# Moving operands of TensorE 128 bytes beyond their stationary ones, modulo 256 bytes, in a three-stage network on one core

## The chip, the cores and the metric

The kernel runs on one core of a Trainium2 chip. The metric is the time of one execution in microseconds, as the device measures it. 1132.77 us is the median of three executions of the kernel before.

## The reference, cut to what matters

Three stages follow each other, for a batch of 2 with 3136 tokens and 256 features. Everything is float32.

```python
# attention: z is 64 wide, v and u are 256 wide
scores = (1.0 / S) * np.matmul(z, z.transpose(0, 2, 1))
attn = np.maximum(scores, 0.0) ** 2
x = u * np.matmul(attn, v)
# layer 1: a token mix of rank 32, then a feed-forward block 256 -> 1024 -> 256
h = x.transpose(0, 2, 1) @ U @ V
u = x + h.transpose(0, 2, 1)
x = u + np.maximum(u @ w_ch1, 0.0) @ w_ch2
# layer 2: a Fourier mix over tokens and features, a normalization, a second block
u = x + np.real(np.fft.fft(np.fft.fft(x, axis=1), axis=2))
un = (u - mean(u)) / np.sqrt(var(u) + 1e-06)
out = u + np.maximum(un @ w_ch1, 0.0) @ w_ch2
```

## The kernel before, in words

Every float32 matrix is split into a high and a low part of type float32r, and a product is the sum of three matmuls: high by high, high by low, low by high. A matmul has a stationary operand (here mostly 128 columns, loaded into the array by an LDWEIGHTS) and a moving one (mostly 448 columns, CH in the code); each matmul loads its own stationary operand, so a load for the next matmul runs beside each matmul.

Tokens go in 7 chunks of 448 per batch element. In attention, `scores` (lines 558 to 595) multiplies blocks of z: stationary KT, moving Q, 64 rows, so that two matmuls, one in the upper and one in the lower half of the array, run side by side as a pair. ScalarE and VectorE make from it the squared scores and split them into `h` and `l`. `products` (lines 599 to 622) multiplies them with the values: stationary Vt, moving `h` and `l`, again in pairs. A chunk has 13 steps, and a full step has 12 pairs of `products` and 3 pairs of `scores`. The 13th block of z has only 64 rows, KTl; its scores are 224 columns wide, the lower half of the array taking the first 224 columns of Q and the upper half the other 224.

In the feed-forward blocks, `hidden` (lines 363 to 376) multiplies the first weights `w` (stationary) with a chunk's `h` and `l`, in six matmuls of 448 columns, and `project` (lines 378 to 397) the second weights with the hidden layer's `Hh` and `Hl`, in another six. Such a step of twelve is repeated 8 times a chunk, for 14 chunks in each layer, and the rest of the program's work (Fourier transforms, normalizations, low-rank sums) is put between these steps by a schedule that is written out by hand. Layer 1's weights are in the pool `wpool`; layer 2's first weights are in `wpool2`, its second ones in `wpool`.

The tiles stand in SBUF one behind the other, pool by pool, in the order in which they are first asked for, without room between them. The sizes of all tiles ahead of a tile therefore set its address. Taken modulo 256 bytes, the address of the moving operand less that of the stationary one (the offset, here) is this when the kernel is built:

| matmuls | moving, stationary | offset before | offset after |
|---|---|---|---|
| attention's scores, line 574 | Q, KT | 0 | 128 |
| the 13th step's scores, lower half, upper half | Q, KTl | 0, 128 | 128, 0 |
| attention's values, line 616 | h or l, Vt | 0 | 128 |
| layer 1, hidden, lines 368 to 370 | h or l, w | 0 | 128 |
| layer 2, hidden, lines 368 to 370 | h or l, w | 64 | 128 |
| both layers, projections, lines 393 to 395 | Hh or Hl, w | 64 | 128 |
| low-rank update, lines 269 and 713 | Vs, Gs | 0 | 128 |
| normalization sums, lines 308 and 327 | sm, ones | 64 | 128 |
| transforms in float32r, lines 956 to 958 and 1013 to 1018 | nh, nl, Th, Tl; b49, fA, fB | 64 | 128 |
| transform in float32, lines 995 and 1005 | f64s; wr, col128 | 64 | 0 |
| low-rank sums in float32, line 234 | xT1, stg or an; Us | 0 to 192 | 0 to 192 |

The 64 in layer 2's hidden matmuls has another origin than that of the projections: there the moving operand is at 0 modulo 256 and the weights are at 192.

The low-rank table `Us` (line 132) holds U for the low-rank sums, `rank_sums` (lines 228 to 238). Its last reader is layer 1's mixer in the middle of the program. `alternating` (lines 926 to 931) makes sums of every second token for the Fourier transform, through a scratch tile `alt` of 1024 bytes per partition.

Of the kernel before, what the change touches and what calls it, by code (L numbers as in the profile page):

```python
# [10 lines left out]
F32 = mybir.dt.float32  # L11
F32R = mybir.dt.float32r
I32 = mybir.dt.int32
# [8 lines left out]
CH = 448  # L22
# [52 lines left out]
def f(ap):  # L75
    return ap.bitcast(F32)
# [3 lines left out]
def program(ctx, tc, zT, v, uT, U, V, w1a, w2a, w1b, w2b, b49, f64, fd, rep, mask, out):  # L80
# [8 lines left out]
    def hcopy(o, i):  # L89
        nc.scalar.copy(o, i)  # L90

    def sub(o, a, b):
        tt(out=o, in0=a, in1=b, op=ALU.subtract)  # L93

    const = ctx.enter_context(tc.tile_pool(name="const", bufs=1))
    com = ctx.enter_context(tc.tile_pool(name="com", bufs=3))
# [34 lines left out]
    ones = const.tile([128, 128], F32R, name="ones")  # L131
    Us = const.tile([128, 26, RANK], F32, name="Us")
    Gs = [const.tile([128, D], F32R, name=f"Gs{b}") for b in range(NB)]

    def constants(t):
        make_identity(nc, ident)
        late_dma(out=repc, in_=rep)
        late_dma(out=maskc[:, 0:7], in_=mask)
        late_dma(out=t[0:98, 0:128], in_=b49)
        late_dma(out=f64s, in_=f64)  # L140
        late_dma(out=t[:, 256:512], in_=fd)
        nc.vector.memset(t[:, 768:896], 1.0 / D)
        for _ in range(3):
            yield
        hcopy(ones, t[:, 768:896])
        for x in (b49h, b49l):
            nc.gpsimd.memset(f(x), 0.0)
        hcopy(b49h[0:98], t[0:98, 0:128])
        sub(b49l[0:98], t[0:98, 0:128], f(b49h[0:98]))
        yield  # L150
        for dst, k in ((fA, 256), (fB, 384)):
            hcopy(dst[:, 0], t[:, k : k + 128])
            sub(dst[:, 1], t[:, k : k + 128], f(dst[:, 0]))
            if dst is fA:
                yield
# [23 lines left out]
    def fetch_w(raw, src, k, second):  # L179
        if second:  # L180
            load(out=raw[:, 0:512], in_=src[k * 128 : k * 128 + 128, :])
        else:
            load(
                out=raw[:, 0:512].rearrange("p (a n) -> p a n", a=2),
                in_=src[:, k * 256 : k * 256 + 256].rearrange("(a p) n -> p a n", p=128),
            )
# [33 lines left out]
    def misc():  # L220
        p, tag = misc_pools[misc_at[0] % len(misc_pools)]
        misc_at[0] += 1
        return p.tile([128, 512], F32, tag=tag, name="ps_" + tag)
# [23 lines left out]
    class Chunk:  # L247
# [2 lines left out]
            self.sl = slice(c * CH, c * CH + CH)  # L250

        def load(self):
            self.vs = com.tile([128, CH], F32R, tag="Vs", name="Vs", bufs=1)
            for k in (0, 64):
                late_dma(out=self.vs[k : k + 64, :], in_=V_d[:, self.sl])

# [142 lines left out]
        def finish(self):  # L399
            b = self.b  # L400
            if self.layer == 1:
                for a in range(2):
                    tt(out=late["xT"][b][:, a, self.sl], in0=self.acc[a][:, 0:CH], in1=self.x[:, a], op=ALU.add)
            else:
                o = c2(ptile())
                if self is chunks[-1]:
                    t0, n = self.c * CH, CH // 2
                    for cuts in (((0, 0, CH),), ((1, 0, n), (1, n, CH))):
                        for a, s, e in cuts:
                            tt(out=o[:, a, s:e], in0=self.acc[a][:, s:e], in1=self.x[:, a, s:e], op=ALU.add)  # L410
                            store = nc.scalar.dma_start if a and s == 0 else load
                            store(out=out[b, a * 128 : a * 128 + 128, t0 + s : t0 + e], in_=o[:, a, s:e])
                    return
                for a in range(2):
                    tt(out=o[:, a], in0=self.acc[a][:, 0:CH], in1=self.rs, op=ALU.mult)
                for a in range(2):
                    tt(out=o[:, a], in0=o[:, a], in1=self.x[:, a], op=ALU.add)
                    load(out=out[b, a * 128 : a * 128 + 128, self.sl], in_=o[:, a])
# [4 lines left out]
    def attention(stack):  # L423
        att = stack.enter_context(tc.tile_pool(name="att", bufs=2))
# [8 lines left out]
        zraw, qraw, vraw = {}, {}, {}  # L433
# [26 lines left out]
                sub(t[:, 1, c : c + 64], raw[:, 0, 0:64], f(t[:, 0, c : c + 64]))  # L460

        def load_q(b, qc):
            t = qraw[b, qc] = att.tile([128, CH], F32, tag="qraw", name="qraw", bufs=1)
            for r in halves[0 : 1 if (b, qc) == (0, 0) else 2]:
                (late_dma if (b, qc) == (0, 1) else load)(out=t[r], in_=zT[b, :, qc * CH : qc * CH + CH])

# [36 lines left out]


        def stage():
            return att.tile([128, 1152], I32, tag="stg", name="stg")

        def conv_U(k):
            raw = stage()
# [223 lines left out]
        t = att.tile([128, 5, D], F32R, tag="an", name="warm", bufs=1).rearrange("p a n -> p (a n)")  # L733
# [7 lines left out]
        for k in range(32):  # L741
            r, n = halves[k % 2], 128 if k < 8 else 352
# [45 lines left out]
        for i in range(-LAG, len(steps)):  # L788
# [3 lines left out]
            if i >= 0:  # L792
                b, qc, p = steps[i]
# [6 lines left out]
                n = i % NP  # L800
# [6 lines left out]
                if (b, qc) == (1, NC - 1):  # L807
                    if p == 2:
                        chunks[0].load()
                        a = att.tile([128, 2, CH], F32, tag="uT", name="uT")  # L810
# [21 lines left out]
    mp = late["mp"] = ctx.enter_context(tc.tile_pool(name="mp", bufs=2))  # L832
# [7 lines left out]
    xT = late["xT"] = [xpool.tile([128, 2, S], F32, tag=f"xT{b}", name=f"xT{b}") for b in range(NB)]  # L840


    raw128 = mp.tile([128, 112], F32, tag="raw128", name="raw128", bufs=1)
    col128 = mp.tile([128, 128], F32, tag="col128", name="col128", bufs=1)
    rows = [mp.tile([128, CH], F32, tag=f"row{k}", name=f"row{k}", bufs=1) for k in range(2)]
    late["half"] = rows[0][:, 0:D]
    y = mp.tile([128, 416], F32, tag="y", name="y", bufs=1)
    top = [mp.tile([98, 32], F32, tag=f"top{b}", name=f"top{b}", bufs=1) for b in range(NB)]
    for t in (raw128, col128, y[:, 392:416]):
        nc.gpsimd.memset(t, 0.0)  # L850
# [8 lines left out]
    def pair_late():  # L859
        nats.append(nats.pop(0))  # L860
        return nats[-1]
# [33 lines left out]
    def halves49(b):  # L895

        nat = {}
        x0, x1 = (xT[b][:, a].rearrange("p (s m r) -> p s m r", m=49, r=2) for a in range(2))
        yv = y[:, 0:392].rearrange("p (s m r) -> p s m r", m=49, r=2)

        def fold(i):

            s0, s1 = 4 * i, 4 * i + 4
            for t0, t1 in ((0, 1), (1, s1)) if s0 == 0 else ((s0, s1),):
                for m, w in ((0, 0), (1, 25), (25, 1)):
                    n = 24 if m else 1
                    in1 = x1[:, t0:t1, w : w + n]
                    if t0:
                        in1 = in1[:, :, :, ::-1]
                    tt(  # L910
                        out=yv[:, t0 - s0 : t1 - s0, m : m + n],
                        in0=x0[:, t0:t1, m : m + n],
                        in1=in1,
                        op=ALU.add,
                    )
            yt = mp.tile([128, 416], F32, tag="A1" if i == 7 else "yt", name="yt", bufs=1)
            nc.vector.transpose(out=yt, in_=y)
            for c in (0, 32, 64, 96):
                (load if c < 64 else late_dma)(
                    out=nat_d[b][i, :, c : c + 32].rearrange("(j t) d -> t j d", t=32),  # L920
                    in_=yt[c : c + 32].rearrange("p (j d) -> p j d", d=32),
                )
            if i == 7:
                load(out=raw128[0:32, 0:98], in_=xT[b][0:1, 1, :].rearrange("o (s p) -> o s p", p=98))

        def alternating(i, x):

            v = x[0:98].rearrange("p (s d r) -> p s d r", s=4, r=2)
            t = mp.tile([98, 4, 64], F32, tag="alt", name="alt", bufs=1)
            sub(t, v[:, :, :, 0], v[:, :, :, 1])  # L930
            nc.vector.reduce_sum(out=top[b][0:98, 4 * i : 4 * i + 4], in_=t, axis=mybir.AxisListType.X)

        def fetch(i):
            h, l = nat[i] = pair_late()
            load(
                out=f(l)[0:98].rearrange("p (s d) -> p s d", s=4),
                in_=nat_d[b][i, 0:392].rearrange("(s p) d -> p s d", p=98),
            )

        def tokens(i):  # L940
            h, l = nat[i]
            hcopy(h[0:98], f(l)[0:98])
            alternating(i, f(l))
            sub(l[0:98], f(l)[0:98], f(h[0:98]))

        def axis49(i):
            ps = misc()
            dft49(ps, *nat.pop(i))
            w = mp.tile([128, 512], F32, tag="wst", name="wst")
            hcopy(w, ps)  # L950
            load(out=scr[b][:, 4 * i : 4 * i + 4, :], in_=w.rearrange("p (s d) -> p s d", s=4))

        return fold, fetch, tokens, axis49

    def dft49(ps, h, l):
        mm(ps, b49h, h, start=True, stop=False)
        mm(ps, b49h, l, start=False, stop=False)  # L957
        mm(ps, b49l, h, start=False, stop=True)  # L958
# [167 lines left out]
    with tc.manual_schedule():  # L1126
# [21 lines left out]
        for i in range(nstep + 2):  # L1148
# [23 lines left out]
            if i in fetches:  # L1172
                b, k0, k1 = fetches[i]
# [57 lines left out]
```

## Time and profile before

| what | value |
|---|---|
| median of three executions | 1132.77 us (1132.64 to 1133.49) |
| the profiled execution's own time | 1132.07 us |
| its span, from the first to the last instruction | 1130.3 us |
| TensorE, matmuls: busy, share of the span | 1125.1 us, 100% |
| VectorE: busy, share | 847.0 us, 75% |
| ScalarE: busy, share | 633.7 us, 56% |
| GpSimd: busy, share | 181.5 us, 16% |
| attention (line 616's last start) | to 536.4 us |
| feed-forward steps of layer 1, then of layer 2 | 536.7 to 835.05 us, then to the end |

In the profile PE is TensorE's matmuls, PEld its weight loads, DVE is VectorE, ACT ScalarE, POOL GpSimd. A matmul's start is measured and its end is modelled, matmuls overlap in the array, and so the time between starts tells the pace, and not the duration that a row gives for one. The chain that ended last goes back from the last instruction to what released each; its shares tell which engine sets the end.

### The profile page before, as it was taken

What the parts mean: (1) busy time and instruction counts of PE and PEld (TensorE: products, weight loads), DVE (VectorE), ACT (ScalarE), POOL (GpSimd) and SP (SyncE); (2) the same over time, 40 slices, a digit from 0 to 9 for tenths busy, and PEclk for the clock granted to TensorE, in tenths of its full rate; (3) what the DMA queues carried; (4) which work ended last, traced back from release to release, by engine and by line L of the source; (5) the groups of instructions that cost most, each with busy time, mean ns of one, the idle gap of its engine ahead of it and who ended that gap; (6) DMA issues with size and microseconds to landing.
All of it is one profiled execution on the core that took longest, in us unless ns stands there. A gap on an engine that the chain in (4) does not pass through costs nothing.

```text
span 1130.3 us, 21424 instructions
## 1 busy us (share of the span) xinstructions
PE 1125.1 (100%) x8310; PEld 1061.7 (94%) x8310; DVE 847.0 (75%) x1571; ACT 633.7 (56%) x1032; POOL 181.5 (16%) x299
## 2 busy tenths in 40 slices
PE   9999999999999999999999999999999999999998
PEld 8999999999999999999989999999999999999997
DVE  8877888888887667676667777577588888777863
ACT  8777777878786666675334444343345444444431
POOL 2202310221022102202221112111131100000010
PEclk9999999999999999999999999999999999999999
DMA  5212322324123302111823455231143321111111
GB/s 168 75 46 61 104 80 69 119 71 127 47 72 118 121 18 59 50 36 32 265 62 95 128 159 130 74 75 45 47 107 100 76 48 42 33 42 33 42 33 42
DMA packets 86758, 88.96 MB, mean 79 GB/s; under 512 B 27398, under 2 KB 76034, under 8 KB 86656
## 3 DMA queue, kind: packets, MB, share of 16 engines
q1 hardware_dynamic: 70272, 58.44, 17.2%
q0 software_dynamic: 16032, 28.93, 10.2%
q8 instruction: 65, 1.06, 0.4%
q14 instruction: 37, 0.30, 0.1%
q10 hardware_dynamic: 352, 0.21, 0.1%
HBM read 57.67 MB, written 29.82 MB: 77 GB/s over the span
## 4 chain that ended last, share of the span: by engine, by line
PE 99%; ACT 0%; DVE 0%; issue 0%; DVEq 0%; POOL 0%; POOLq 0%
PE psO L616 37%; PE psS L574 9%; PE psH L368 8%; PE psH L369 8%; PE psC L394 8%; PE psC L395 8%; PE psH L370 8%; PE psC L393 8%; PE psS L743 0%; PE ps_m L995 0%; PE ps_g L995 0%; PE ps_x L995 0%; PE psS L234 0%; PE ps_g L234 0%; PE ps_m L958 0%; PE ps_m L957 0%
## 5 line engine op out<-in xcount | busy, mean ns | idle before, releaser
L616 PE MATMUL psO<-h,Vt 64*128 64x448 f32 x2744 | 345.1, 363 | 0.2 <-DVE h L585 0.2
L616 PEld LDWEIGHTS psO<-h,Vt 64*128 64x128 f32 x2744 | 294.4, 185 | 9.1 <-DVE h L585 0.7
L93 DVE TENSOR_TENSOR l<-P,h 128x896 fp32r<-128x896 f32 (+2 forms) x237 | 224.8, 954 | 33.3 <-ACT h L90 16.4
L373 ACT ACTIVATE Hh<-psH 128x448 fp32r<-128x448 f32 x224 | 121.0, 541 | 201.5 <-PE psH L370 198.3
L374 DVE SCALAR_TENSOR_TENSOR Hl<-psH,Hh 128x448 fp32r<-128x448 f32 x224 | 138.3, 620 | 117.9 <-ACT Hh L373 115.7
L590 ACT ACTIVATE P<-psS 128x896 f32<-128x896 f32 (+1 forms) x181 | 160.2, 885 | 85.4 <-PE psS L574 84.6
L616 PE MATMUL psO<-l,Vt 64*128 64x448 f32 x1372 | 206.4, 363 | 0.0
L592 DVE CAST h<-P 128x896 fp32r<-128x896 f32 (+1 forms) x181 | 110.9, 613 | 85.0 <-ACT P L591 83.8
L591 ACT ACTIVATE P<-P 128x896 f32<-128x896 f32 (+1 forms) x181 | 167.4, 925 | 5.7
L368 PE MATMUL psH<-h,w 128*128 128x448 f32 x448 | 166.5, 372 | 0.0
L616 PEld LDWEIGHTS psO<-l,Vt 64*128 64x128 f32 x1372 | 159.9, 185 | 4.4 <-DVE l L93 0.3
L369 PE MATMUL psH<-l,w 128*128 128x448 f32 x448 | 163.4, 365 | 0.0
L394 PE MATMUL psC<-Hl,w 128*128 128x448 f32 x448 | 163.4, 365 | 0.0
L370 PE MATMUL psH<-h,w 128*128 128x448 f32 x448 | 162.9, 364 | 0.0
L393 PE MATMUL psC<-Hh,w 128*128 128x448 f32 x448 | 162.9, 364 | 0.0
L395 PE MATMUL psC<-Hh,w 128*128 128x448 f32 x448 | 162.7, 363 | 0.0
L574 PE MATMUL psS<-Q,KT 64*128 64x448 f32 x1002 | 147.6, 364 | 0.0
L574 PEld LDWEIGHTS psS<-Q,KT 64*128 64x128 f32 x1002 | 115.2, 185 | 3.7 <-issue 0.4
L368 PEld LDWEIGHTS psH<-h,w 128*128 128x128 f32 x448 | 84.3, 188 | 7.9 <-issue 0.3
L393 PEld LDWEIGHTS psC<-Hh,w 128*128 128x128 f32 x448 | 84.2, 188 | 6.8 <-issue 0.2
L370 PEld LDWEIGHTS psH<-h,w 128*128 128x128 f32 x448 | 84.2, 188 | 6.5
L394 PEld LDWEIGHTS psC<-Hl,w 128*128 128x128 f32 x448 | 84.2, 188 | 6.3 <-DVE Hl L374 0.5
(313 smaller groups left out, 1157.1 us busy)
## 6 DMA issues: line engine op xcount, KB each, us to landing
out<-P SPq DMA_DIRECT2D x27, 224.0 KB, 1.9
uT<-in_uT SPq DMA_DIRECT2D x13, 448.0 KB, 4.0
aTd<-aT POOLq DMA_DIRECT2D x13, 448.0 KB, 3.1
aNd<-aT POOLq DMA_DIRECT2D x104, 56.0 KB, 2.4
vraw<-in_v SPq DMA_DIRECT2D x18, 256.0 KB, 2.7
scr<-wst SPq DMA_DIRECT2D x16, 256.0 KB, 2.0
Vs<-Vd POOLq DMA_DIRECT2D x28, 112.0 KB, 2.6
xT<-aTd SPq DMA_DIRECT2D x7, 448.0 KB, 4.6
```

Source lines behind the costliest of these rows:

```text
L93: tt(out=o, in0=a, in1=b, op=ALU.subtract)
L368: mm(ps[:, 0:CH], wh, self.h[:, a], start=a == 0, stop=False)
L369: mm(ps[:, 0:CH], wh, self.l[:, a], start=False, stop=False)
L370: mm(ps[:, 0:CH], wl, self.h[:, a], start=False, stop=a == 1)
L374: stt(out=l, in0=ps[:, 0:CH], scalar=0.0, in1=f(h), op0=ALU.max, op1=ALU.subtract)
L393: mm(dst, wh, h, start=k == 0, stop=False)
L394: mm(dst, wh, l, start=False, stop=False)
L395: mm(dst, wl, h, start=False, stop=k == 7)
L574: mm(dst[:, 0:w], k, q[r, kq, o : o + w], start=(kk, kq) == (0, 0), stop=kk == 1)
L590: act(out=A[:, x].rearrange("p (a n) -> p a n", a=2), in_=ps[:, :, 0:w], func=AF.Relu, scale=1.0 / S)
L591: act(out=A[:, x], in_=A[:, x], func=AF.Square)
L616: mm(o[fa][i][:, 0:CH], vt[r, j, k, fa * 128 : fa * 128 + 128], x[r, j * CH : j * CH + CH], start=p == 0 and fa not in [t[1][0] for t in t ...
```

## The change

Some tiles get spare columns, which moves every tile behind them, and one scratch tile goes elsewhere:

- an unused tile `gap` of 128 bytes behind `Gs` moves the pools that follow by 128 bytes;
- `Vs` and `qraw` get 32 columns more, of which the first 448 are used;
- the staging tile `stg` gets 16 columns more;
- `raw128` has 128 columns instead of 112, and its fill with zeros is 16 columns longer;
- the scratch of `alternating` is now the first 256 columns of `Us`, seen as one row, and the tile `alt` falls away.

The offsets that result are in the table above. Each engine issues the same instructions in the same order and with the same waits; besides addresses, only the fill of `raw128` and the name of the scratch tile differ.

```diff
@@ -131,6 +131,7 @@
     ones = const.tile([128, 128], F32R, name="ones")
     Us = const.tile([128, 26, RANK], F32, name="Us")
     Gs = [const.tile([128, D], F32R, name=f"Gs{b}") for b in range(NB)]
+    const.tile([128, 32], F32, name="gap")
@@ -250,7 +251,7 @@
         def load(self):
-            self.vs = com.tile([128, CH], F32R, tag="Vs", name="Vs", bufs=1)
+            self.vs = com.tile([128, CH + 32], F32R, tag="Vs", name="Vs", bufs=1)[:, 0:CH]
             for k in (0, 64):
@@ -460,7 +461,7 @@
         def load_q(b, qc):
-            t = qraw[b, qc] = att.tile([128, CH], F32, tag="qraw", name="qraw", bufs=1)
+            t = qraw[b, qc] = att.tile([128, CH + 32], F32, tag="qraw", name="qraw", bufs=1)[:, 0:CH]
@@ -503,7 +504,7 @@
         def stage():
-            return att.tile([128, 1152], I32, tag="stg", name="stg")
+            return att.tile([128, 1168], I32, tag="stg", name="stg")
@@ -840,11 +841,12 @@
-    raw128 = mp.tile([128, 112], F32, tag="raw128", name="raw128", bufs=1)
+    raw128 = mp.tile([128, 128], F32, tag="raw128", name="raw128", bufs=1)
     col128 = mp.tile([128, 128], F32, tag="col128", name="col128", bufs=1)
...
     y = mp.tile([128, 416], F32, tag="y", name="y", bufs=1)
+    spare = Us.rearrange("p a n -> p (a n)")
     top = [mp.tile([98, 32], F32, tag=f"top{b}", name=f"top{b}", bufs=1) for b in range(NB)]
     for t in (raw128, col128, y[:, 392:416]):
         nc.gpsimd.memset(t, 0.0)
@@ -926,7 +928,7 @@
             v = x[0:98].rearrange("p (s d r) -> p s d r", s=4, r=2)
-            t = mp.tile([98, 4, 64], F32, tag="alt", name="alt", bufs=1)
+            t = spare[0:98, 0:256].rearrange("p (s d) -> p s d", s=4)
             sub(t, v[:, :, :, 0], v[:, :, :, 1])
             nc.vector.reduce_sum(out=top[b][0:98, 4 * i : 4 * i + 4], in_=t, axis=mybir.AxisListType.X)
```

## Rows read from the trace of the kernel before

**Rows 1.** The page, busy time of each engine.
```profile
PE 1125.1 (100%) x8310; PEld 1061.7 (94%) x8310; DVE 847.0 (75%) x1571; ACT 633.7 (56%) x1032; POOL 181.5 (16%) x299
```
**Rows 2.** The page, chain that ended last, shares by engine.
```profile
PE 99%; ACT 0%; DVE 0%; issue 0%; DVEq 0%; POOL 0%; POOLq 0%
```
**Rows 3.** The page, costliest groups: count after x, then busy us, mean ns.
```profile
L616 PE MATMUL psO<-h,Vt 64*128 64x448 f32 x2744 | 345.1, 363 | 0.2 <-DVE h L585 0.2
...
L616 PE MATMUL psO<-l,Vt 64*128 64x448 f32 x1372 | 206.4, 363 | 0.0
...
L368 PE MATMUL psH<-h,w 128*128 128x448 f32 x448 | 166.5, 372 | 0.0
...
L395 PE MATMUL psC<-Hh,w 128*128 128x448 f32 x448 | 162.7, 363 | 0.0
L574 PE MATMUL psS<-Q,KT 64*128 64x448 f32 x1002 | 147.6, 364 | 0.0
```
**Rows 4.** Busy us by stretch: PE, PEld, DVE, ACT, POOL, granted clock, DMA.
```profile
100.00:500.00 400.00, 400.00 (x3985) 389.29 (x3985) 311.70 (x470) 291.72 (x388) 66.32 (x98) 1.00 0.25 75
836.00:1125.00 289.00, 289.00 (x1464) 268.41 (x1463) 220.67 (x480) 121.74 (x254) 34.11 (x61) 1.00 0.20 52
```
**Rows 5.** Chain in order of time, attention: start us, us, what.
```profile
46.63 2.43 PE psO L616 x18
49.05 0.61 PE psS L574 x5
49.67 2.43 PE psO L616 x18
52.09 0.61 PE psS L574 x5
52.71 2.43 PE psO L616 x18
55.13 0.61 PE psS L574 x4
55.75 2.43 PE psO L616 x18
```
**Rows 6.** Timeline of PE in layer 1: start us, us, instruction; 72 lie between.
```profile
549.51 0.36 PE L368 MATMUL psH<-h,w 128*128 128x448 f32 x1
...
564.07 0.36 PE L368 MATMUL psH<-h,w 128*128 128x448 f32 x1
```
**Rows 7.** Timeline of PE in layer 2; 60 lie between.
```profile
1109.28 0.36 PE L368 MATMUL psH<-h,w 128*128 128x448 f32 x1
...
1121.34 0.37 PE L368 MATMUL psH<-h,w 128*128 128x448 f32 x1
```
**Rows 8.** Timeline of PE, three matmuls of 512 columns and the next.
```profile
700.73 0.39 PE L956 MATMUL ps_g<-nh,b49h 128*128 128x512 f32 x1
700.95 0.39 PE L957 MATMUL ps_g<-nl,b49h 128*128 128x512 f32 x1
701.18 0.40 PE L958 MATMUL ps_g<-nh,b49l 128*128 128x512 f32 x1
701.41 0.37 PE L368 MATMUL psH<-h,w 128*128 128x448 f32 x1
```
**Rows 9.** Timeline of PE, a 13th step's scores and the next.
```profile
20.59 0.49 PE L574 MATMUL psS<-Q,KTl 64*128 64x224 f32 x6
20.92 1.79 PE L616 MATMUL psO<-h,Vt 64*128 64x448 f32 x16
```
**Rows 10.** Timeline of PE, matmuls of 64 columns and the next.
```profile
711.97 0.28 PE L957 MATMUL ps_g<-nl,b49h 128*128 128x64 f32 x1
712.08 0.28 PE L958 MATMUL ps_g<-nh,b49l 128*128 128x64 f32 x1
712.19 0.45 PE L368 MATMUL psH<-h,w 128*128 128x448 f32 x1
```
**Rows 11.** Tiles alt and Us: durations ns min/median/max, first and last start.
```profile
L93 DVE TENSOR_TENSOR alt<-nl x16: 404/416/427, 636.2 to 854.9; 98x256 f32<-98x256 f32 x16
...
L238 PE MATMUL ps_g<-row,Us x8: 218/218/219, 572.0 to 572.1; 128*32 128x64 f32 x8
```

## The prediction

> **What bounds the kernel now.** I read the page first: TensorE is busy for 1125.1 of the 1130.3 us span, VectorE for 75% of it [rows 1], and 99% of the chain that ended last is TensorE [rows 2]. Nothing else has to be waited for, so only a change of TensorE's own pace can move the end. The costliest groups say how much work goes at that pace [rows 3]: line 616 issues 2744 + 1372 = 4116 half-array matmuls and line 574 issues 1002; the two halves of the array work side by side, so these are 2559 pairs. The feed-forward layers issue six groups of 448 full-array matmuls (the first and the last are shown), 2688 in all. Each moves 448 columns, which at the 2.4 GHz level (granted clock 1.00 in both stretches, [rows 4]) is 186.7 ns.
>
> The actual pace is what the rest rests on, so I took it from starts, not from the modelled ends. In attention, with moving and stationary operand at offset 0, the chain in order of time shows a step of 15 pairs each 3.04 us: 46.63 to 55.75 is three steps, 9.12 us for 45 pairs, **202.7 ns** [rows 5]. In layer 1 six steps of twelve matmuls run without extra work from 549.51 to 564.07: 14.56 us for 72, 202.2 ns [rows 6]. In layer 2 five such steps run from 1109.28 to 1121.34: 12.06 us for 60, **201.0 ns** [rows 7]. The same lines, shapes and engines; what differs is that layer 1's hidden matmuls have offset 0 and layer 2's have 64, while the projections have 64 in both. If the projections go at 201.0 in both, layer 1's hidden matmuls take 2 x 202.2 - 201.0 = **203.4 ns**. So offset 0 costs 202.7 to 203.4 ns in two unrelated places, offset 64 costs 201.0, and both are 14 to 17 ns above the columns. That excess belongs to a matmul, not to its columns: the 512-column matmuls of line 956 to 958 take 0.68 us for three, 227 ns, 13 ns above their 213.3 [rows 8].
>
> I read this as the weights' read for the next matmul getting in the way of the running matmul's moving read, a little less often at offset 64 than at 0. The Trainium skill speaks against it: "TensorE: Matmul & The Clock Gate", Part 2 ("What happens when you issue a matmul"), says that the moving operand and the weights come through two independent read ports and that loading the next weights takes no read bandwidth from the running matmul. By that rule the offset could not matter and the time would stay; the 1.2 ns per matmul between [rows 6] and [rows 7] speaks for an effect, though not for its cause.
>
> **The change, part by part.** Instructions, their order on every engine and their waits stay as they were; only addresses differ.
>
> 1. *Attention*, 2559 pairs from offset 0 to 128. No row shows a 448-column matmul with offset 128 under way for long, so its pace must be bounded. Below: the columns alone, 186.7 ns. Above: 203.4 ns, the worst pace at any offset here [rows 6], if 128 acts as 0 does. The one group that has 128 now decides nothing: the upper half's matmuls of the 13th step (KTl, 224 columns, lower half at 0) take 0.33 us for three pairs, 110 ns [rows 9], but matmuls of only 64 columns also follow each other at 110 ns [rows 10], so weight loads alone set that. I take the nearest rows and go on in a line: 64 bytes saved 1.7 ns (202.7 to 201.0) to 2.4 ns (203.4 to 201.0), so about 2 ns, and 64 more save about 2 again: **199.0 ns**. Gain 2559 x 3.7 = 9.5 us; the ends give -41 us (16.0 ns each) and +1.8 us (0.7 ns each).
> 2. *Layer 1 hidden*, 672 matmuls from 0 to 128: 672 x 4.4 = 3.0 us; ends -11.2 us (16.7 ns) and nothing.
> 3. *Layer 2 hidden and all projections*, 672 + 1344 = 2016 matmuls from 64 to 128: 2016 x 2.0 = 4.0 us; ends -28.8 us (14.3 ns) and +4.8 us (2.4 ns).
> 4. *KTl matmuls*: 42 pairs at the pace of the weight loads; nothing. Their halves only change places, since the upper half is now at 0. The transform and low-rank matmuls are some 200, at 2 ns 0.4 us; left out.
> 5. *The scratch tile in Us*: the subtraction and the sum that used the tile `alt` keep their lengths. The new neighbour is the low-rank table's last reader, line 238 at 572.1 us; the first use of the scratch is at 636.2 us [rows 11], 64 us later, and the tile had one buffer before too, so no wait is added and nobody is queued behind one. VectorE has room (it is off the chain). Nothing.
> 6. *Spare columns*: 16 more columns in one fill on GpSimd, once; nothing, as nothing of it is on the chain [rows 2].
>
> Sum: 9.5 + 3.0 + 4.0 = 16.5 us. The profiled execution took 1132.07 us, of which the span is 1130.3; that gives 1115.6, and against the median of the runs, 1132.77 (0.7 above the profiled one), **1116 us**. What is late next: in attention VectorE works 311.7 of 400 us [rows 4], 78%; at a pace faster by 2% it would stand at 80%, so it does not take over, and in layer 2 it is at 220.7 of 289 us, 76%.
>
> **The rivals.**
>
> *A. The pattern repeats every 128 bytes (slower).* Then 128 is the same as 0, attention and layer 1 gain nothing, and the 2016 matmuls that stand at 64 today lose what they had: 2016 x 2.4 = 4.8 us, **1137.6 us**. For it: two points, 0 and 64, cannot tell a slope from half a period, and [rows 9] show no advantage at 128. Against it: nothing in the trace; that is why it weighs much. It decides as soon as the pace at 128 is above 202.1 ns, where the 2016 x 1.1 ns = 2.2 us lost are as much as attention (2559 x 0.6 ns) and layer 1's hidden matmuls (672 x 1.3 ns) give. If 128 lay beyond 0 by as much as 64 lies below it (205 ns), the terms would be 5.9 + 1.1 + 8.1 us, 1148.
>
> *B. The collision goes away altogether.* If two reads meet only when both stand in the same half of 256 bytes, 128 would take away all of the excess: the lower ends of 1 to 3, 41 + 11 + 29 = 81 us, **1052 us** at the very best; with half of the excess gone, 1092. For it: the excess is 14 ns, far more than the 2 ns that 64 bytes gave. Against it: shifting a quarter of 256 bytes took only an eighth of the excess, and most of it may be a cost of handing over from one matmul to the next that no offset removes. The Trainium skill, "TensorE: Matmul & The Clock Gate", section "Back-to-back issue gap", gives 2.5 ns above the columns, for 448 an estimate of 189.2 ns; by that the time would be about 1063 us, and no row here shows such a pace.
>
> *C. 64 is enough.* The pace at 128 is that at 64: 2559 x 1.7 + 672 x 2.4 = 6.0 us, **1126.8 us**. Nothing in the profile excludes it.
>
> *D. The offset does nothing.* Layer 2's hidden weights lie in another pool, far from layer 1's; the 14 ns per step could come from there, or from the other work beside it. Then the time stays at **1132.8 us**. That is what the rule of the Trainium skill quoted above would have. Against: attention's weights lie elsewhere again and run at the pace of layer 1's.
>
> **How the numbers follow.** The forecast (the line goes on, more or less: 1095 to 1122) has 0.37; A, with all that ends slower, 0.27; B, or most of it (below 1095), 0.13; C 0.12; D 0.11. What a measurement of this kernel tells from no change is about 0.2%, 2.3 us. Faster by more than that: 0.37 + 0.13 + 0.12 = 0.62; slower 0.27; between 0.11. The range for 8 in 10 takes in A at its price with a margin (1140) and, downward, B with some two thirds of the excess gone (1080). The forecast's own range is 1095 to 1122.
>
> **What would show it.** The starts tell: an attention step of 15 pairs should fall from 3.04 to about 2.99 us, and a step of twelve feed-forward matmuls should take the same 2.39 us in layer 1 and layer 2 (now 2.43 and 2.41). Equal paces in both layers would show that the offset set their difference; 2.43 us in both is A, 2.41 in both is C, 2.30 or less is B, 2.43 and 2.41 as before is D. VectorE's groups must keep their lengths, and no new wait of TensorE may appear; if one does, or if the 512-column matmuls of line 956 move otherwise than the rest, the reasoning is wrong whatever the sum.

## The result and the profile after

The changed kernel takes **1140.34 us** (median of four executions, 1140.12 to 1140.79) where the kernel before takes 1132.73 in the same comparison: the ratio is **1.0066**, 95% interval 1.0049 to 1.0084. It is slower by 7.6 us; the forecast was 1116. The profiled execution took 1140.16 us, its span is 1138.4.

The page of the changed kernel, busy time of each engine, and the shares of the chain that ended last:

```profile
PE 1133.2 (100%) x8310; PEld 1063.9 (93%) x8310; DVE 847.0 (74%) x1571; ACT 634.7 (56%) x1032; POOL 180.6 (16%) x299
...
PE 99%; ACT 0%; DVE 0%; issue 0%; DVEq 0%; POOL 0%; POOLq 0%
```

Against [rows 1] and [rows 2] only TensorE has changed by more than some 2 us: the same 8310 matmuls, 8.1 us more busy time, VectorE at the same 847.0 us, and the chain is TensorE's alone as before. So nothing new is waited for; the matmuls themselves follow each other more slowly. The chain in order of time, in attention (start us, us, what):

```profile
46.58 2.45 PE psO L617 x24
49.03 0.61 PE psS L575 x6
49.63 2.45 PE psO L617 x24
52.09 0.61 PE psS L575 x6
52.70 2.45 PE psO L617 x24
55.15 0.61 PE psS L575 x6
55.76 2.45 PE psO L617 x24
```

46.58 to 55.76 is 9.18 us for 45 pairs, 204.0 ns, where [rows 5] gave 202.7. The timeline of TensorE, five plain feed-forward steps of layer 1 and five of layer 2 (start us, us, instruction; 60 matmuls from the first row of a pair to the second):

```profile
551.54 0.37 PE L369 MATMUL psH<-h,w 128*128 128x448 f32 x1
...
563.78 0.37 PE L369 MATMUL psH<-h,w 128*128 128x448 f32 x1
...
1117.10 0.36 PE L369 MATMUL psH<-h,w 128*128 128x448 f32 x1
...
1129.34 0.36 PE L369 MATMUL psH<-h,w 128*128 128x448 f32 x1
```

Both are 12.24 us for 60, 204.0 ns; [rows 6] and [rows 7] gave 202.2 and 201.0. The layers' difference is gone, as the forecast wanted it as a sign that the offset sets the pace, but at 2.45 us a step and not at 2.39. Busy time by stretch (PE, PEld, VectorE, ScalarE, GpSimd, granted clock, DMA share, GB/s), with counts of matmuls, shows the same in another way:

```profile
100.00:500.00 400.00, 400.00 (x3975) 387.59 (x3973) 310.96 (x470) 291.44 (x388) 65.40 (x98) 1.00 0.26 75
836.00:1125.00 289.00, 289.00 (x1445) 265.12 (x1444) 222.49 (x484) 123.28 (x256) 35.02 (x61) 1.00 0.19 52
```

In the same 400 and 289 us as [rows 4] the granted clock is 1.00 again (the level of 2.4 GHz), and 3975 and 1445 matmuls start, where [rows 4] have 3985 and 1464.

**Where the 7.6 us come from.** For all that follows I took the mean time from one start to the next over the whole trace, for matmuls of 448 columns, leaving out gaps of 225 ns and more (other work between). Attention went from 202.96 to 203.94 ns, the feed-forward layers from 201.72 to 203.92. 2559 x 1.0 + 2688 x 2.2 = 2.5 + 5.9 = 8.4 us. The two profiled executions differ by 8.1 us (1132.07 and 1140.16), the medians by 7.6; so the paces account for the loss.

### The profile page after: what moved, and what is told of

It reads as the page before. It is cut to its first block, busy times and chain, and to the rows that moved or that the text cites. A ratio compares the mean times of both kernels' runs of the same rounds, so it can differ in the third digit from the quotient of the medians.

```text
span 1138.4 us, 21424 instructions
## 1 busy us (share of the span) xinstructions
PE 1133.2 (100%) x8310; PEld 1063.9 (93%) x8310; DVE 847.0 (74%) x1571; ACT 634.7 (56%) x1032; POOL 180.6 (16%) x299
## 4 chain that ended last, share of the span: by engine, by line
PE 99%; ACT 0%; DVE 0%; issue 0%; DVEq 0%; POOL 0%; POOLq 0%
PE psO L617 37%; PE psS L575 9%; PE psH L369 8%; PE psC L395 8%; PE psH L371 8%; PE psC L396 8%; PE psC L394 8%; PE psH L370 8%; PE psS L744 0%; PE ps_m L997 0%; PE ps_g L997 0%; PE ps_x L997 0%; PE psS L235 0%; PE ps_g L235 0%; PE ps_m L959 0%; PE ps_m L960 0%
## 5 line engine op out<-in xcount | busy, mean ns | idle before, releaser
L617 PE MATMUL psO<-h,Vt 64*128 64x448 f32 x2744 | 333.4, 363 | 0.2 <-DVE h L586 0.2
L617 PEld LDWEIGHTS psO<-h,Vt 64*128 64x128 f32 x2744 | 283.6, 184 | 9.2 <-DVE h L586 0.7
L93 DVE TENSOR_TENSOR l<-P,h 128x896 fp32r<-128x896 f32 (+2 forms) x237 | 224.7, 953 | 33.3 <-ACT h L90 16.5
L617 PE MATMUL psO<-l,Vt 64*128 64x448 f32 x1372 | 192.8, 362 | 0.0
L617 PEld LDWEIGHTS psO<-l,Vt 64*128 64x128 f32 x1372 | 148.7, 184 | 4.1 <-DVE l L93 0.2
L575 PE MATMUL psS<-Q,KT 64*128 64x448 f32 x1002 | 137.6, 364 | 0.0
L575 PEld LDWEIGHTS psS<-Q,KT 64*128 64x128 f32 x1002 | 106.4, 184 | 3.5 <-issue 0.4
```

Of the source, the lines that this page charges most:

```text
L575: mm(dst[:, 0:w], k, q[r, kq, o : o + w], start=(kk, kq) == (0, 0), stop=kk == 1)
L617: mm(o[fa][i][:, 0:CH], vt[r, j, k, fa * 128 : fa * 128 + 128], x[r, j * CH : j * CH + CH], start=p == 0 and fa not in [t[1][0] for t in t ...
```

## The experiments

**One distance at a time.** The forecast drew a line through two points. The first question is therefore the pace at each distance by itself. Each of these kernels is the changed one with the moving operands of all matmuls of 448 and 512 columns placed D bytes beyond the stationary ones modulo 256; the sizes of the spare columns and an unused tile `gap2` (none at 0) are the only edit. For D = 64 (lines that change, without those between):

```diff
-    const.tile([128, 32], F32, name="gap")
+    const.tile([128, 16], F32, name="gap")
-            self.vs = com.tile([128, CH + 32], F32R, tag="Vs", name="Vs", bufs=1)[:, 0:CH]
+            self.vs = com.tile([128, CH + 48], F32R, tag="Vs", name="Vs", bufs=1)[:, 0:CH]
+            if b == 0:
+                att.tile([128, 48], F32, name="gap2", bufs=1)
-            t = qraw[b, qc] = att.tile([128, CH + 32], F32, tag="qraw", name="qraw", bufs=1)[:, 0:CH]
+            t = qraw[b, qc] = att.tile([128, CH + 16], F32, tag="qraw", name="qraw", bufs=1)[:, 0:CH]
-            return att.tile([128, 1168], I32, tag="stg", name="stg")
+            return att.tile([128, 1152], I32, tag="stg", name="stg")
-    raw128 = mp.tile([128, 128], F32, tag="raw128", name="raw128", bufs=1)
+    raw128 = mp.tile([128, 112], F32, tag="raw128", name="raw128", bufs=1)
-            e = mp.tile([57, 64], F32, tag="ech", name="ech", bufs=1)
+            e = mp.tile([57, 80], F32, tag="ech", name="ech", bufs=1)[:, 0:64]
```

For other D the gap has D/4 columns (none at 0) and the rest follows. What was expected of 64, 0 and 192:

> All matmul groups that the change moved to offset 128 are at offset 64 instead (stationary operands at 0 modulo 256, moving ones at 64). Theory 1, the pace follows the offset: 201.0 ns everywhere, attention 2559 x 1.7 and layer 1's hidden matmuls 672 x 2.4 ns faster than before, 1126 to 1127 us. Theory 2, the absolute place of a tile or its pool sets the pace: attention stays at 202.7 to 204 ns and the time at 1132 to 1140 us.

> All at offset 0. Theory 1, the pace follows the offset: 202.7 to 203.4 ns everywhere, the projections and layer 2's hidden matmuls lose 2016 x 2.4 ns = 4.8 us against before, 1137 to 1138 us, a little faster than the changed kernel (1140.3). Theory 2, absolute place: no rule; the two layers would differ by some 14 ns per step of twelve, as before the change.

> All at offset 192. If the pace has a period of 128 bytes in the offset, 192 acts as 64: 201 ns, 1126 to 1127 us. If the period is 256 and the pace goes up again past 64 (201 at 64, 203 at 0, 204 at 128), 192 is the worst: 205 to 208 ns, 1145 to 1160 us. If 64 and 192 mirror each other around 128 in a collision that is worst at 128, it is 201 ns again; then only a finer step tells.

And then of the places between:

> All at offset 32. Theory 1, a smooth curve over 256 bytes with its best place near 64 (203 ns at 0, 200.0 at 64, 204.0 at 128, 202.3 at 192): 201.4 ns, halfway, about 1128 us. Theory 2, the read comes in pieces of 64 bytes and only the piece counts: 203 ns as at 0, 1138 us.

> All at offset 96. Theory 1, a smooth curve: 202 ns, halfway between 200.0 at 64 and 204.0 at 128, about 1131 us. Theory 2, pieces of 64 bytes: 200 ns as at 64, 1121 us. If the best place lies between 64 and 128, under 200 ns and under 1120 us.

> All at offset 160. Theory 1, a smooth curve: 203.1 ns, halfway between 204.0 at 128 and 202.3 at 192, about 1136 us. Theory 2, pieces of 64 bytes: 204 ns as at 128, 1140 us.

> All at offset 224. The offsets that are odd multiples of 32 gave 205 ns (32 and 96) and 200 to 203 ns (160). If the curve is the same shifted by 128, 224 goes with 160 at 200 to 203 ns, 1125 to 1132 us; if it goes with 32 and 96, 205 ns and 1145 to 1147 us.

Measured (mean ns from start to start; the times are medians, the ratio is against the kernel before with its 95% interval):

```
distance      attention  feed-forward  time us   ratio (interval)
before (mix)  202.96     201.72        1132.7    1
0             203.10     203.33        1137.94   1.0044 (1.0032 to 1.0055)
32            204.18     205.14        1145.77   1.0115 (1.0086 to 1.0145)
64            200.08     200.11        1120.66   0.989  (0.9873 to 0.9906)
96            205.28     205.28        1147.49   1.0131 (1.0101 to 1.016)
128 (change)  203.94     203.92        1140.34   1.0066 (1.0049 to 1.0084)
160           202.53     201.42        1132.36   0.9994 (0.9982 to 1.0005)
192           202.17     202.20        1131.37   0.9984 (0.9973 to 0.9994)
224           203.85     203.99        1141.1    1.0068 (1.0045 to 1.0091)
```

Every row's time follows from its paces to within 1.5 us: from 64 to 96 it is 26.8 us for 5.2 ns, some 5160 matmuls' worth, and the program has 2559 + 2688 = 5247. Only the row of 0 came out as one of its theories had it; the others lie off all that was expected of them. The curve is neither a line nor one of period 128 (64 and 192 differ by 2.1 ns, 32 and 160 by 1.7 and 3.7). The one place that is good all through is narrow: 64 lies between two of the worst, 32 and 96. **All at 64 beats both kernels**: 1120.66 us, the ratio to before is 0.989. The chain in order of time of that kernel (the same columns; its attention lines stand two later than the changed kernel's), and its timeline in layer 2:

```profile
46.73 2.40 PE psO L619 x24
49.13 0.60 PE psS L577 x6
...
55.73 2.40 PE psO L619 x24
```

```profile
1099.07 0.36 PE L369 MATMUL psH<-h,w 128*128 128x448 f32 x1
1099.27 0.36 PE L370 MATMUL psH<-l,w 128*128 128x448 f32 x1
...
1101.47 0.36 PE L369 MATMUL psH<-h,w 128*128 128x448 f32 x1
```

9.00 us for 45 pairs and 2.40 us for twelve matmuls: 200.0 ns in both. Its busy time from 100 to 500 us tells why VectorE did not take over:

```profile
100.00:500.00 400.00, 399.76 (x4041) 378.10 (x4039) 317.14 (x477) 296.32 (x394) 66.87 (x99) 1.00 0.26 77
```

VectorE works 317 of the 400 us, 79%, at a pace 1.4% above that of before, still with room.

**Distance or absolute place?** In the kernel above the weights stand at 0 and what moves at 64. The same distance with the weights at 64 and the moving operands at 128, the place that they have in the changed kernel (an update's, the normalization's and the transforms' few matmuls keep 128 as distance):

```diff
     const.tile([128, 32], F32, name="gap")
...
-            self.vs = com.tile([128, CH + 32], F32R, tag="Vs", name="Vs", bufs=1)[:, 0:CH]
+            self.vs = com.tile([128, CH + 48], F32R, tag="Vs", name="Vs", bufs=1)[:, 0:CH]
...
```

The other lines are those of D = 64. Only `gap` is not made smaller, and so all that lies behind it stands 64 bytes further.

> Offset 64 as in the run before with all at 64, but both operands stand 64 bytes further (stationary at 64, moving at 128 modulo 256); the low-rank update, normalization sums and transforms, some 100 matmuls, are at 128. If only the offset counts, the pace is 201 ns as with all at 64, 1126 to 1128 us. If the place of the moving operand counts, it is that of the changed kernel, whose moving operands are at 128 too: 204 ns, 1139 to 1141 us.

1121.92 us (ratio 0.9901, 0.9882 to 0.9921), 200.1 ns in attention and in the feed-forward layers as with the weights at 0, most steps 2400 ns. Moving operands at 128 give 203.9 ns over weights at 0 and 200.1 over weights at 64: the distance counts, not the place.

**Distance to which weights?** A matmul runs with weights loaded earlier, while those of the next one are loaded beside it. In layers where all weights stand alike the two distances are the same. Two kernels tell them apart: all at 64 as above, but layer 2's first weights alone lie 32 (then 128) bytes further, so that its hidden matmuls have 32 (192) and the projections keep 64. Where the stage changes, the last hidden matmul has its own weights at the new distance and the next ones, a projection's, at 64; the last projection has it the other way round.

```diff
-            e = mp.tile([57, 80], F32, tag="ech", name="ech", bufs=1)[:, 0:64]
+            e = mp.tile([57, 88], F32, tag="ech", name="ech", bufs=1)[:, 0:64]
```

(Against the kernel with all at 64; 112 in place of 88 for the second. Widening this tile moves what lies behind it: the pool of those weights, `xT`, which among matmuls only the low-rank sums read, and some tiles that no matmul reads.)

> All at offset 64 but layer 2's first weights, which stand 32 bytes further; no other tile of a matmul moves, and the moving operands stay at 64. Layer 2's hidden matmuls so have offset 32 (64 - 32). Theory 1, the distance to the weights counts: layer 1's step stays at 2.400 us, layer 2's goes to some 2.43 us (six gaps of 205.1 instead of 200.1 ns), 672 x 5.0 ns = 3.4 us, 1124 us. Theory 2, the weights' place plays no part: 2.400 us in both layers, 1120 to 1121 us. If the matmul that runs beside a load counts, the gap behind a step's last projection is long and the one behind its last hidden matmul short; if a matmul's own weights count, the other way round.

> As the run before, with layer 2's first weights 128 bytes further than with all at 64: offset 192 (64 - 128). Theory 1, the distance to the weights counts: layer 2's step 2.41 us (six gaps of 202.2 ns), 672 x 2.1 ns = 1.4 us, 1122 us. Theory 2, the weights' place plays no part: 2.400 us, 1120 to 1121 us.

The timeline of the first of them, one step of layer 2:

```profile
1106.66 0.36 PE L369 MATMUL psH<-h,w 128*128 128x448 f32 x1
1106.86 0.37 PE L370 MATMUL psH<-l,w 128*128 128x448 f32 x1
1107.06 0.37 PE L371 MATMUL psH<-h,w 128*128 128x448 f32 x1
1107.27 0.37 PE L369 MATMUL psH<-h,w 128*128 128x448 f32 x1
1107.48 0.37 PE L370 MATMUL psH<-l,w 128*128 128x448 f32 x1
1107.68 0.36 PE L371 MATMUL psH<-h,w 128*128 128x448 f32 x1
1107.89 0.37 PE L394 MATMUL psC<-Hh,w 128*128 128x448 f32 x1
1108.09 0.36 PE L395 MATMUL psC<-Hl,w 128*128 128x448 f32 x1
1108.29 0.36 PE L396 MATMUL psC<-Hh,w 128*128 128x448 f32 x1
1108.49 0.36 PE L394 MATMUL psC<-Hh,w 128*128 128x448 f32 x1
1108.69 0.36 PE L395 MATMUL psC<-Hl,w 128*128 128x448 f32 x1
1108.89 0.37 PE L396 MATMUL psC<-Hh,w 128*128 128x448 f32 x1
1109.10 0.36 PE L369 MATMUL psH<-h,w 128*128 128x448 f32 x1
```

The step takes 2.44 us. The projections run at 200 ns up to the last, 1108.89, behind which 210 ns pass. Behind the last hidden matmul, 1107.68, 210 ns pass in this step too. The hidden matmuls vary by 10 ns from one to the next, so I go by the means over some 50 steps (ns from start to start; the last line is the median):

```
                                          moved by 32   moved by 128
first five hidden (own and next: 32/192)     205.7         201.8
last hidden (own 32/192, next 64)            201.0         201.6
first five projections (own and next 64)     200.9         199.7
last projection (own 64, next 32/192)        205.0         206.7
layer 1, a step of twelve                   2400          2400
```

In the first column the last hidden matmul is fast and the last projection slow. **This speaks for the distance from the moving operand to the weights that are loaded beside it, the next matmul's**, and against the distance to its own. In the second column the last projection is slow again (206.7, more than the 202.2 of 192), and the last hidden one, where 192 and 64 lie close, decides nothing. The kernels took 1124.77 and 1123.32 us (one execution each), and layer 1 keeps its 2400 ns.

Two things limit this. Single gaps differ by their place in a step even where all distances are alike: the projections of the second kernel average 200.9, 197.5 and 201.6 ns by turns. Against the same places in the kernel with all at 64 (200.9 ns behind the last hidden matmul and behind the last projection of layer 2) it is the last projection alone that is clearly slower, in both kernels. And all moving operands stand at 64 here, so the slow gap could also belong to the matmul that follows, by its own two operands. The kernel before speaks against a rule of a matmul's own operands: in its layer 2 all twelve have 64, and a step takes 2412 ns [rows 7] and not 2400. There the last hidden matmul has 0 to the projection's weights, and the last projection 128 to the next hidden ones. In its layer 1 the gap behind the last hidden matmul, with 0 to the next weights, is 202.6 ns and the one behind the last projection, with 64, is 200.8, though the matmuls that follow have 64 and 0 of their own. But single gaps show it only in part (behind the first projection of layer 1 205.4 ns pass, behind the last hidden matmul of layer 2 200.1), and layer 2's hidden operands stand at 0 over weights at 192, a place that was not tried with all alike. So the next weights are the best reading of the runs, and not shown beyond doubt.

**Is it how much the load reads?** If the two reads got in each other's way byte by byte, a shorter load should leave more of the moving read alone. In the kernel before, four of the six hidden matmuls of a step load 32 columns of weights and no longer 128 (left out: 96 of 128 hidden units of the corrections for the low halves):

```diff
-                mm(ps[:, 0:CH], wh, self.h[:, a], start=a == 0, stop=False)
-                mm(ps[:, 0:CH], wh, self.l[:, a], start=False, stop=False)
-                mm(ps[:, 0:CH], wl, self.h[:, a], start=False, stop=a == 1)
+                if a == 0:
+                    mm(ps[:, 0:CH], wh, self.h[:, a], start=True, stop=False)
+                mm(ps[0:32, 0:CH], wh[:, 0:32], self.l[:, a], start=False, stop=False)
+                mm(ps[0:32, 0:CH], wl[:, 0:32], self.h[:, a], start=False, stop=False)
+                if a == 1:
+                    mm(ps[:, 0:CH], wh, self.h[:, a], start=False, stop=True)
```

> The kernel before, but four of the six hidden matmuls of each step have 32 stationary columns instead of 128: the low-part corrections of 96 of every 128 hidden units are left out. If the 14 to 17 ns above the columns come from the weight load beside a matmul, the starts after a matmul with a short load beside it are 187 to 191 ns apart and the step of twelve falls by four times 10 to 14 ns, to about 2.37 to 2.39 us. If they are a cost of handing over from one matmul to the next, every gap stays at 200 to 204 ns and the step at 2.43 us (layer 1).

The weight loads grouped by line (count: ns min/median/max, first to last start; shape):

```profile
L370 PEld LDWEIGHTS psH<-l,w x448: 107/108/112, 538.0 to 1123.7; 128*32 128x32 f32 x150
L373 PEld LDWEIGHTS psH<-h,w x224: 187/188/188, 538.8 to 1124.1; 128*128 128x128 f32 x112
```

The short load takes 108 ns for 188, and the gaps of 187 to 191 ns that would have shown it as the cause do not come: 202.7 ns between hidden matmuls, a step most often 2.420 us (before: 2.427 in layer 1, 2.413 in layer 2), 1133.98 us in all (one execution). The load's length is not what costs here.

At distance 64 the same edit was tried in three forms: as above, with all four short loads from columns 8 to 40 (32 bytes further), and with only the third hidden matmul's short load from there.

> All at offset 64, and four of the six hidden matmuls of a step have 32 stationary columns (the low-part corrections of 96 of every 128 hidden units are left out). If a load's length plays no part at this offset either, a step stays at 2.400 us and the time at 1120 to 1122 us; if it does, the step falls by 20 to 50 ns.

> As the run before, but the 32 stationary columns begin 8 columns, 32 bytes, further, so that these four matmuls have offset 32 with the moving operands where they were. Theory 1, the start of the weights against the start of the moving operand sets the pace: four or five gaps of a step go from 200 to some 205 ns, the step to 2.42 us and the time to 1125 to 1127 us. Theory 2, the weights play no part and only where the moving operands stand among the tiles does: 2.400 us and 1120 to 1122 us.

> As the run with short loads at offset 64, but only the third of the six hidden matmuls has its weights 32 bytes further. If it matters whose moving read runs while these weights are loaded, the gap ahead of this matmul (second to third start) changes; if it matters how a matmul's own two operands stand, the gap behind it (third to fourth) does. One gap of 200 becomes about 205 ns, the step 2.405 us; if neither changes, the weights' place plays no part.

These gave 1124.31, 1124.52 and 1125.03 us (one execution each), with mean steps of 2417, 2421 and 2420 ns where long loads take 2400. In the first, hidden matmuls took 202.8 ns and projections 200.0. Shorter loads made the good place worse, which I had not expected. By the rule of the next weights, 32 bytes on four of twelve should add 20 ns to the step of the first form, and 4 came. In the third form one gap was to grow by 5 ns; against the first form, the gap ahead of the third hidden matmul went from 204.4 to 203.4 ns and the one behind it from 201.8 to 202.0. So the rule does not hold as it stands for short loads, and why they are slower at 64 stays open.

## Why the prediction was wrong

**The step that failed** is in points 1 to 3: "I take the nearest rows and go on in a line". 64 bytes saved some 2 ns, so 64 more were to save 2 again, 199.0 ns. Measured at 128 are 203.9 ns, more than at 0. With 203.94 and 203.92 ns in place of 199.0 the three terms change sign. Point 1 was -9.5 us and is +2.5; points 2 and 3 together were -7.0 and are +5.9, nearly all of it from the 2016 matmuls that stood at 64, the best place of the eight, and were moved away from it.

**The rate at 64 was mis-sized too.** I took the 201.0 ns of [rows 7] for the pace at 64. By the rule of the next weights a step of layer 2 of before is a mixture: its first weights stand at 192, so ten of the twelve have 64, but the last hidden matmul has 0 to the projection's weights, and the last projection 128 to the next hidden ones. With the paces of the table that gives (10 x 200.1 + 203.3 + 203.9) / 12 = 200.7 ns, 0.6 of the 0.9 ns by which the 201.0 read lies above 200.1. So 64 saves 3 ns, and rival C ("64 is enough", 1126.8 us) would really have been 1120.7.

**The rivals.** A, the pattern that repeats every 128 bytes, was right in sign, and its reason for weight, that two points cannot tell a slope from half a period, is what happened; its price of 1137.6 us was 2.7 us low. Its mechanism falls, as the eight distances show; its note that 128 might lie beyond 0 came nearer (203.9 against 203.1 to 203.3; I had put 205). The forecast gave the slower side 0.27 although nothing in the trace spoke against it; a line through two points deserved no more than that. B falls: no distance comes nearer than 13.3 ns to the 186.7 of the columns (the 1063 us beside it, from a figure that no run here shows, would be some 1065 by the paces of points 1 to 3). D falls with the layers' equal paces.

**What held.** TensorE's pace alone moved the end. Order and waits stayed: the tile that moved into the low-rank table costs nothing, as its rows in the changed kernel show (ns min/median/max, first to last start; compare [rows 11]):

```profile
L93 DVE TENSOR_TENSOR Us<-nl x16: 403/414/428, 638.9 to 859.2; 98x256 f32<-98x256 f32 x16
...
L239 PE MATMUL ps_g<-row,Us x8: 219/219/219, 574.2 to 574.3; 128*32 128x64 f32 x8
```

The 512-column matmuls, moved from 64 to 128 like the projections, went with the rest, in the mean of 16 groups of three from 229 to 233 ns. One of these groups in the changed kernel, whose starts, 698.27 to 698.97, are 233 ns apart against the 227 of [rows 8]:

```profile
698.27 0.40 PE L958 MATMUL ps_m<-nh,b49h 128*128 128x512 f32 x1
698.51 0.39 PE L959 MATMUL ps_m<-nl,b49h 128*128 128x512 f32 x1
698.74 0.39 PE L960 MATMUL ps_m<-nh,b49l 128*128 128x512 f32 x1
698.97 0.36 PE L270 MATMUL ps_x<-Vs,Gs 128*128 128x448 f32 x1
```

**What did not hold beside it.** The prediction has the excess belong to a matmul and not to its columns, from the one group of [rows 8], 13 ns above its 213.3. The mean of the 16 groups is larger for 512 columns than for 448: with all at 64 it is 229.8 ns, 16.5 above the columns where 448 have 13.4, and in the changed kernel 232.9, 19.6 where 448 have 17.2. An excess that grows with the columns would be 15.3 and 19.7. So the runs rather speak for the columns; 16 groups do not decide it.

**The reading behind it** was that the read of the next weights gets in the way of the running matmul's moving read. That the next weights' place has a part is what the runs speak for (205.0 and 206.7 ns behind a last projection whose own weights stand at 64), with the limits said above. The Trainium skill, "TensorE: Matmul & The Clock Gate", Part 2 ("What happens when you issue a matmul"), has two independent read ports and no bandwidth lost to the load; by that rule all eight distances would have one pace. They differ by up to 5.2 ns, and the measurement decides, for this kind of matmul and load. That the two reads meet in SBUF is not shown, and the shorter load speaks against a cost that grows with what the load reads. What happens inside is open: why 64 is best, why 32 and 96 are worst, and what makes the 13.3 ns that remain at 64. A matmul without a load beside it was not tried, nor were distances between multiples of 32.

## What to carry to other kernels

Where TensorE is 99% of the chain and every matmul has its own weight load, take the pace from start to start and try the placement of the moving operand relative to the next weights, in steps of 32 bytes over 256: here one place of eight was worth 1.1% against before and a neighbour cost 1.3%. Two points of such a curve say nothing about a third; when a change goes to a value that no row shows, the other sign has to weigh as much as the line does. Place the weights of stages that alternate alike: with layer 2's first weights 32 bytes off the good place the kernel took 1124.8 us and not 1120.7, and the matmul ahead of the change of stage was slow too.

## What the runs showed of the hardware that was not expected

- Around 64, a shift of 32 bytes changes a matmul's pace by 4 to 5 ns (200.1 at 64; 205.1 at 32 and 205.3 at 96 in the feed-forward layers), and at no distance tried is the mean for 448 columns below 200.0 ns, 13.3 above the columns.
- The gaps repeat in short cycles. In the changed kernel they are 203, 212, 200, 209 and 196 ns, 1020 for five; at 64 they are 197, 202 and 201, 600 for three, and a step of twelve takes 2400 ns in 102 of the 105 that have no gap of 225 ns or more.
- The pace of one distance is a mean over such cycles. At 160 a step takes 2400 ns, as at 64, in 68 of all 118, and 2480 in 23, many in a row; two steps of either kind follow. That may be why attention and the feed-forward layers differ by 1 ns at 32 and 160. What chooses between the cycles is open.

```profile
554.24 0.36 PE L369 MATMUL psH<-h,w 128*128 128x448 f32 x1
...
559.04 0.36 PE L369 MATMUL psH<-h,w 128*128 128x448 f32 x1
...
592.73 0.37 PE L369 MATMUL psH<-h,w 128*128 128x448 f32 x1
...
597.69 0.37 PE L369 MATMUL psH<-h,w 128*128 128x448 f32 x1
```

- A weight load of 32 columns has a record of 108 ns in place of 188 and doesn't bring the next matmul sooner; at distance 64 four such loads made the step of twelve longer by 17 ns.
